# A transformer block with modulated norms: sums moved by some 30 slots, a normalisation moved from ScalarE to GpSimd, and two product chunks of the tail handed out later

## The chip, the cores and the metric

The kernel runs on one core of a Trainium2 chip. A core has five engines that run their own instruction queues and meet through semaphores: TensorE (PE in the profile), VectorE (DVE), ScalarE (ACT), GpSimd (POOL) and SyncE (SP), which here only issues DMAs. The metric is the time of one execution on the device in microseconds (us), as the median of several runs.

## The reference, cut to what matters

One transformer block for 2048 rows of width 512, with six modulation vectors made from a condition `c`:

```python
mod = (_silu(c) @ w_mod).reshape(c.shape[0], 6, 1, -1)
sa, ca, ga, sb, cb, gb = (mod[:, j] for j in range(6))
h = _layernorm(x, axis=-1) * (1 + ca) + sa
x = x + ga * _A_ref(h, A_k_cache, A_v_cache, A_wq, A_wo)      # attention, 32 heads, 8 of K and V, the last 512 keys
h = _layernorm(x, axis=-1) * (1 + cb) + sb
x = x + gb * _B_ref(h, B_w_gate, B_w_up, B_w_down)            # (gelu(h @ w_gate) * (h @ w_up)) @ w_down
```

The change touches three places of it: the making of `sb` and `cb` (modulations 3 and 4), the second layernorm `(x - mean) / sqrt(var + eps)` of the first 1024 rows, and the last down products of the feed-forward.

## The kernel before, in words

Every large product is done in float16 halves: an operand is split into a high and a low part, and `mm3` (lines 85 to 88) issues three 128x512 matmuls for one product of 128 contracted elements. The scale of each operand comes from bounds on its norm, which is why there are many small scale steps.

**Attention** is a list of 512 score tiles, run in a loop over "slots" t = 0 to 511 with a few more at the end. In each slot PE makes the scores of one tile (`ps`), DVE takes their row maximum (`nm`, L945), ACT the exponential (`ee`, L954), and for the tiles of two and three slots ago ACT and DVE make the high and low half of the probabilities `p` (L966 and L971), which a transposing DMA turns into `pt`. PE also takes three further pieces of work from a list in each slot: query products, value products (`po`) and output products (`py`), whose results DVE and ACT turn into `qt`, `ot` and the accumulator `acc` (L705, L706, L914). The first 256 slots serve rows 0 to 1023 (first half), the others the rest (second half). In the first half the weights are also split and stored, in the second most of them are fetched back.

**The order** of this loop is written out by hand: within it each engine executes what the code issues, in the order in which it issues it. Side work has slots: `at(t, f)` and `at(("w", t), f)` put f at the end of slot t, `sched` gives a load and its later steps their slots, and a planner spaces the loads by the free buffers (five `raw` buffers of 256 KB) and issues them on SP, with about one background DMA in a slot. The rest of the feed-forward, behind the loop, is not in hand order: there a scheduler orders the instructions of PE, DVE, ACT and GpSimd; only SP's stay as written.

**Modulation.** For modulations 3, 4 and 5 a column block of `w_mod` is loaded as a 128x512 tile (`wmc`, `mod_load`), and `mod_col` (L135) multiplies it by silu(c) and sums along the row on DVE; for modulation 4 a one is added (L137). When the eight columns of 3 and 4 are there, `mod_max` (L189) takes their largest value and `mod_scale` (two small transposes on PE at L194, then L196 to L211 on DVE) scales them for the feed-forward. Their first readers are the affine steps of the second layernorm.

**Second layernorm.** When the attention output of a 128-row tile of rows 0 to 1023 is complete (`attn_final`), its accumulator is stored to `y1`, and `ln_tile(2, ...)` runs on it in place: `stat` (mean and variance on DVE, the power on GpSimd at L386, one slot later), `norm` (six slots later), `turn` (four transposes on PE at L495, eight slots later), the affine (L503 on ACT), its store to `hs` and the split into the blocks `b` (L521 on ACT, L523 on GpSimd). There are eight such tiles, at slots about 258 to 294.

**Tail.** The feed-forward goes through 28 steps q, each of seven products named by `ORDER` (L1527). Pairs of steps (gate and up) give eight output chunks of six matmuls each (`py<-wo,at`), kept in the list `nexty`; `y_next()` issues one. At four of the seven places of each step one chunk of an earlier pair is issued; what is left is issued behind the last step.

Of the kernel before, what the change touches and what calls it, by code (L numbers as in the profile page):

```python
# [10 lines left out]
F32 = mybir.dt.float32  # L11
F16 = mybir.dt.float16
BF16 = mybir.dt.bfloat16
AF = mybir.ActivationFunctionType
ALU = mybir.AluOpType
AX = mybir.AxisListType

P = 128
# [45 lines left out]
def block_kernel(ctx: ExitStack, tc: tile.TileContext, x, kT, v, wq, wo, wg, wu, wd, cT, wc, wm, out):  # L64
    nc = tc.nc
# [3 lines left out]
    small = ctx.enter_context(tc.tile_pool(name="small", bufs=4))  # L69
# [3 lines left out]
    def tmp(name):  # L73
        return pool.tile([P, 512], F32, tag="e", name=name, bufs=NE)

    def raw(name):
        return pool.tile([P, 512], F32, tag="raw", name=name, bufs=NRAW)
# [4 lines left out]
    def bank(tag, name, bufs):  # L82
        return psum.tile([P, 512], F32, tag=tag, name=name, bufs=bufs)
# [8 lines left out]
    def dma(out_, in_):  # L92
        moved[0] += 1
        nc.sync.dma_start(out_, in_)
# [81 lines left out]
    def col(name, i=0):  # L176
        return ST[name][:, i:i + 1]

    def ts(out, src, a, b=None, op0=ALU.mult, op1=ALU.mult):
        if b is None:  # L180
            nc.vector.tensor_scalar(out, src, a, None, op0=op0)
        else:
            nc.vector.tensor_scalar(out, src, a, b, op0=op0, op1=op1)

    def little(name, n=1, bufs=4, dtype=F32):
        return small.tile([P, n], dtype, tag=name, name=name, bufs=bufs)

    def absmax(out, src):
        nc.vector.tensor_reduce(out, src, axis=AX.X, op=ALU.max, apply_absolute_value=True)  # L189

    def everywhere(out, m, n, fold=True):
        ps = bank("acc", "pst", NACC)
        for i in range(n):
            nc.tensor.transpose(ps[:, i * P:(i + 1) * P], m[:, i:i + 1].to_broadcast([P, P]), ident)  # L194
        src = ps[:, :n * P] if fold else ps[:, :n * P].rearrange("p (n q) -> p n q", n=n)
        nc.vector.tensor_reduce(out, src, axis=AX.X, op=ALU.max)  # L196

    def mod_max(j):
        m = little("mm", 2, 1)
        absmax(m, cols[:, j:j + 2, :])  # L200
        return m

    def mod_scale(j, name, const_, m=None, mid=nop, between=nop):
        m, g, s = m or mod_max(j), little("mg", 2, 1), little("ms", 1, 1)
        everywhere(g, m, 2, False)
        mid()
        nc.vector.tensor_tensor(s, g[:, 0:1], g[:, 1:2], op=ALU.add)
        ts(s, s, FLOOR, RT / TOP13, ALU.max)
        ts(col(name), s, const_)
        between()  # L210
        nc.vector.reciprocal(s, s)  # L211
        ts(cols[:, j:j + 2, :], cols[:, j:j + 2, :], s)
# [23 lines left out]
    def pool_ts(out, src, a, b=1.0, op0=ALU.mult, op1=ALU.mult):  # L236
        nc.gpsimd.tensor_scalar(out, src, a, b, op0=op0, op1=op1)
# [108 lines left out]
    def spilled(gen, key):  # L346
        if (gen, key) not in hs:
            n = KT if key in (0, 1) else 2
            hs[gen, key] = dram.tile([P, n, QB], F32, name=f"hs{gen}_{key}")
        return hs[gen, key]  # L350
# [20 lines left out]
    def ln_cols(key):  # L371
        return (1, 0) if key == "a" else (4, 3)

    def ln_stat(a, st, act=False):
        bn = small.tile([P, 6], F32, name="bn")
        nc.vector.bn_stats(bn, a)
        st["mv"] = small.tile([P, 2], F32, name="mv")
        nc.vector.bn_aggr(st["mv"], bn)
        st["rs"] = small.tile([P, 1], F32, name="rs")
        nc.vector.tensor_scalar(st["rs"], st["mv"][:, 1:2], EPS, None, op0=ALU.add)  # L380
        if act:
            st["nm"] = small.tile([P, 1], F32, name="nmean")
            nc.vector.tensor_scalar(st["nm"], st["mv"][:, 0:1], -1.0, None, op0=ALU.mult)

    def ln_power(st):
        nc.gpsimd.tensor_tensor(st["rs"], st["rs"], nhalf, op=ALU.pow)  # L386
# [58 lines left out]
    def put_off(n, fn):  # L445

        waits_.append([n, fn])
# [17 lines left out]
    def ln_tile(gen, i, src):  # L465
        jsc, jsh = ln_cols("a" if gen < 2 else "f")
        qb, i = divmod(i % (2 * QT), QT)
        st = {}

        def load():  # L470
            if gen == 2:
                st["x"] = src()
            else:
                st["x"] = raw("xs")
                dma(st["x"], src())

        def stat():
            ln_stat(st["x"], st)
            ln_power(st)
            if gen == 2:  # L480
                st["nm"] = small.tile([P, 1], F32, name="nmean")
                pool_ts(st["nm"], st["mv"][:, 0:1], st["rs"], -1.0)

        def norm():
            if gen == 3:
                rs, nm = col("kmax", qb * QT + i), col("kinv", qb * QT + i)
                return nc.scalar.activation(st["x"], st["x"], AF.Identity, bias=nm, scale=rs)
            if gen == 2:
                return nc.scalar.activation(st["x"], st["x"], AF.Identity, bias=st["nm"], scale=st["rs"])
            nc.vector.tensor_scalar(st["x"], st["x"], st["mv"][:, 0:1], st["rs"], op0=ALU.subtract, op1=ALU.mult)  # L490

        def turn():
            st["ps"] = bank("acc", "pln", NACC)
            for dt in range(KT):
                nc.tensor.transpose(st["ps"][:, dt * P:(dt + 1) * P], st["x"][:, dt * P:(dt + 1) * P], ident)  # L495

        def affine(dts):
            if 0 in dts:
                st["f"] = raw("hf") if gen == 2 else tmp("hf")
            f = st["f"]  # L500
            for dt in dts:
                sl = slice(dt * P, (dt + 1) * P)
                nc.scalar.activation(f[:, sl], st["ps"][:, sl], AF.Identity,  # L503
                                     scale=cols[:, jsc, dt:dt + 1], bias=cols[:, jsh, dt:dt + 1])
            if KT - 1 in dts:
                def spill():
                    dma(spilled(gen, qb)[:, :, i * P:(i + 1) * P], f.rearrange("p (k q) -> p k q", k=KT))

                if gen == 3:
                    put_off(3, spill)  # L510
                else:
                    spill()

        def parts(act):
            o = slice(i * P, (i + 1) * P)
            f = st["f"].rearrange("p (k q) -> p k q", k=KT)
            for h, name in enumerate(("b11", "b21") if qb == 0 else (None, "b22")):
                if name:
                    t, src = block(gen, name), f[:, 2 * h:2 * h + 2, :]
                    if act:  # L520
                        nc.scalar.activation(t[:, 0:2, o], src, AF.Copy)  # L521
                    else:
                        nc.gpsimd.tensor_tensor(t[:, 2:4, o], src, t[:, 0:2, o], op=ALU.subtract)  # L523

        more = [lambda: parts(True), lambda: parts(False)] if gen < 3 else []
        return load, [nop if gen == 3 else stat, norm, turn, lambda: affine((0, 1)), lambda: affine((2, 3))] + more
# [170 lines left out]
    def at(key, *fns):  # L697
        later.setdefault(key, []).extend(fns)
# [425 lines left out]
    for dt in range(KT):  # L1124
        sched(6 + dt, (lambda dt=dt: gate_load(dt), [lambda dt=dt: gate_cols(dt)]), ahead=8)
    at(("d", 10), lambda: ts(cols[:, 2, :], gps["ps"][:, 0:KT], 1.0, None, ALU.mult))
    for j, ts_ in ((3, (211, 215, 223, 227)), (4, (213, 217, 225, 229)), (5, (274, 278, 282, 286))):
        for dt in range(KT):
            box = {}
            sched(ts_[dt], (lambda box=box, j=j, dt=dt: box.update(f=mod_load(j, dt)), [lambda box=box: box["f"]()]))  # L1130
    at(11, lambda: mod_row(2))
    mx = {}
    at(("w", 232), lambda: mx.update(m=mod_max(3)))
    at(234, lambda: mod_scale(3, "mf", 1.0, mx["m"]))

    def sched_combos(gen, p, base):
        for k, (load, steps) in enumerate(combos(gen, p, nc.gpsimd if gen or p == 0 else nc.vector, False, 0 if gen else 1 if p else 2, 0 if gen or p else 5)):
# [77 lines left out]
    NQ = 4 * NP  # L1215
# [323 lines left out]
    for i in range(2 * QT):  # L1539
        load, steps = ln_tile(3, i, lambda i=i: y1[2 * QT + i])  # L1540
        q = 7 * (2 + i // 2) + 3 * (i % 2)
# [3 lines left out]
    for p in range(2):  # L1545
        q = 7 * (7 + 2 * p)
# [13 lines left out]
    for q in range(NQ):  # L1560
        n, m = divmod(q, 2)
        its = items(NG + q) if q < 2 else f_items(q)
        for k, pk in enumerate(ORDER):
            if (q, pk) not in f_done:
                all_of(its[pk])
            run(("f", q, k))
            tick()
            if k in (1, 2, 5, 6):
                y_next()
        if m == 1:  # L1570
            for qi, (a, b) in enumerate((("11", "21"), ("12", "22"))):
                for i in range(QT):
                    nexty.append(y_tasks((2 * (n // NP) + qi) * QT + i, [lambda n=n, a=a: A[n, a], lambda n=n, b=b: A[n, b]],
                                         [("f", n, 0), ("f", n, 1)], col("dysc", n % NP), f_final if n % NP == NP - 1 else None))
# [39 lines left out]
```

## Time and profile before

| what | value |
|---|---|
| runs | 1769.34, 1772.45, 1772.27 us; median 1772.27 |
| the profiled execution | 1769.1 us, of which the span of the profile is 1767.3 |
| granted TensorE clock | 1.0 |
| PE waits in all, for `qt` alone | 15.4 us, 12 times |
| the eight normalisations on ACT (L489) | 0.815 us each (median), 708 to 786 us |
| the twelve modulation sums on DVE (L135) | 0.683 us each (median), 1.642 the longest |

All times in the profile are from the start of the span. "Busy" is the time in which an engine has an instruction in work; PE's matmuls overlap, so the 0.38 us of one and the 0.215 us from one start to the next are both right. A group row names line, engine, operation, output <- inputs, shapes and count, then busy us and mean ns, then the idle time in front and who ended it. In a timeline row the numbers are start and duration, and a bracket at the end is the idle time of that engine in front of it, with the releaser. The releaser is inferred; where it had long been done, another was meant.

### The profile page before, as it was taken

The page shows a single profiled execution, that of the slowest core. Times are in us where ns is not written, and L with a number is a line of the kernel's source. Part 1 is how long each engine was busy: PE and PEld are TensorE (multiplying, and loading weights), DVE is VectorE, ACT ScalarE, POOL GpSimd, SP SyncE. Part 2 cuts the span into 40 slices and gives each one's busy share as a digit, 9 for nine tenths or more (in the row PEclk, how much of TensorE's full clock was granted, in tenths as well). Part 3 has the DMA queues.
Part 4 walks back from the last instruction along what each step waited for, and adds up shares of the span by engine and source line. Part 5 has one row for each costly group of instructions (what it writes and reads, how often), then busy time and mean ns, then how long its engine had stood idle before and what let it go on. Part 6 is the DMA issues. An engine that isn't in the chain of part 4 may idle for free.

```text
span 1767.3 us, 25992 instructions
## 1 busy us (share of the span) xinstructions
PE 1730.0 (98%) x8114; PEld 796.3 (45%) x8114; DVE 1447.2 (82%) x2501; ACT 1219.3 (69%) x2830; POOL 882.2 (50%) x1119
## 2 busy tenths in 40 slices
PE   7899999999999999999999999999999999999998
PEld 4444444444444444444444444444444444444443
DVE  7888888888888998888888888888886768767676
ACT  5887787878778777897777777777674555434342
POOL 4879878776788873444565555555520024000000
PEclk9999999999999999999999999999999999999999
DMA  7999999989999997999999999999985643252222
GB/s 230 209 195 210 218 217 200 223 204 221 216 216 227 224 201 145 208 205 234 208 208 208 212 214 204 206 211 214 188 185 131 199 129 114 83 173 90 86 75 75
DMA packets 662122, 327.62 MB, mean 185 GB/s; under 512 B 553056, under 2 KB 575840, under 8 KB 661984
## 3 DMA queue, kind: packets, MB, share of 16 engines
q1 hardware_dynamic: 661696, 325.44, 80.0%
q8 instruction: 64, 1.05, 0.3%
q14 instruction: 74, 0.61, 0.1%
q10 hardware_dynamic: 288, 0.52, 0.1%
HBM read 131.73 MB, written 59.90 MB: 108 GB/s over the span
## 4 chain that ended last, share of the span: by engine, by line
PE 72%; DVE 14%; ACT 8%; issue 3%; POOL 2%; DMA 1%; SPq 0%; ACTq 0%; POOLq 0%; DVEq 0%
PE py L86 7%; PE py L88 7%; PE py L87 7%; DVE p L971 5%; PE ps L86 4%; PE ps L88 4%; PE ps L87 4%; PE po L86 4%; PE po L88 4%; PE po L87 4%; DVE nm L945 3%; PE fa L86 3%; PE fa L88 3%; PE fa L87 3%; ACT ee L954 2%
## 5 line engine op out<-in xcount | busy, mean ns | idle before, releaser
L954 ACT ACTIVATE ee<-ps,nm 128x512 f32<-128x512 f32 x512 | 350.9, 685 | 251.0 <-DVE nm L945 245.6
L971 DVE SCALAR_TENSOR_TENSOR p<-ee,rr,p 128x512 f16<-128x512 f32 x512 | 470.0, 918 | 0.9 <-ACT p L966 0.7
L945 DVE TENSOR_REDUCE nm<-ps 128x1 f32<-128x512 f32 x512 | 349.4, 683 | 77.0 <-PE ps L88 75.5
L966 ACT ACTIVATE p<-ee,rr 128x512 f16<-128x512 f32 x512 | 365.4, 714 | 2.3 <-DMA pt<-p 1.9
L86 PE MATMUL ps<-k,qt 128*128 128x512 f16 x512 | 194.1, 379 | 16.6 <-DVE qt L706 15.4
L86 PE MATMUL py<-wo,ot 128*128 128x512 f16 x512 | 194.1, 379 | 4.4 <-DVE ot L706 4.4
L87 PE MATMUL po<-pt,v 128*128 128x512 f16 x512 | 194.0, 379 | 0.0
L88 PE MATMUL po<-pt,v 128*128 128x512 f16 x512 | 194.0, 379 | 0.0
L87 PE MATMUL py<-wo,ot 128*128 128x512 f16 x512 | 194.0, 379 | 0.0
L88 PE MATMUL py<-wo,ot 128*128 128x512 f16 x512 | 194.0, 379 | 0.0
L86 PE MATMUL po<-pt,v 128*128 128x512 f16 x512 | 194.0, 379 | 0.0
L88 PE MATMUL ps<-k,qt 128*128 128x512 f16 x512 | 194.0, 379 | 0.0
L87 PE MATMUL ps<-k,qt 128*128 128x512 f16 x512 | 193.9, 379 | 0.0
L962 DVE RECIPROCAL rr<-rr 128x2 f32<-128x2 f32 x256 | 41.4, 162 | 99.6 <-ACT rr L959 98.5
L87 PEld LDWEIGHTS <-w 128*128 128x128 f16 x728 | 71.2, 98 | 86.2 <-issue 1.2
L88 PEld LDWEIGHTS <-w 128*128 128x128 f16 x728 | 71.2, 98 | 86.0 <-issue 0.2
L86 PEld LDWEIGHTS <-w 128*128 128x128 f16 x728 | 71.2, 98 | 85.5 <-DVE w L1016 0.3
L914 DVE SCALAR_TENSOR_TENSOR acc<-py,dysc,acc 128x512 f32<-128x512 f32 x112 | 81.6, 747 | 31.5 <-PE py L88 30.5
L954 ACT ACTIVATION_READ_ACCUMULATOR ee<-ps,nm 128x1 f32 x512 | 100.8, 197 | 0.0
L914 DVE SCALAR_TENSOR_TENSOR acc<-py,ysc,acc 128x512 f32<-128x512 f32 x128 | 94.7, 740 | 3.9 <-PE py L88 3.9
L706 DVE SCALAR_TENSOR_TENSOR ot<-po,ot 128x512 f16<-128x512 f32 x128 | 87.0, 680 | 0.0
L86 PE MATMUL py<-wo,at 128*128 128x512 f16 x224 | 84.9, 379 | 1.4 <-DVE at L1263 1.4
(270 smaller groups left out, 3765.9 us busy)
## 6 DMA issues: line engine op xcount, KB each, us to landing
w<-kept SPq DMA_DIRECT2D x123, 256.0 KB, 3.2
wo<-kept SPq DMA_DIRECT2D x60, 256.0 KB, 3.5
raw<-in_wo SPq DMA_DIRECT2D x56, 256.0 KB, 3.1
kept<-stage SPq DMA_DIRECT2D x56, 256.0 KB, 3.3
kept<-w SPq DMA_DIRECT2D x39, 256.0 KB, 3.4
rw<-in_wq SPq DMA_DIRECT2D x38, 256.0 KB, 3.3
hs<-hf SPq DMA_DIRECT2D x32, 256.0 KB, 2.7
pt<-p SPq DMA_TRANSPOSE x512, 3.5
```

The costliest lines, as they stand in the source:

```text
L86: nc.tensor.matmul(ps, llo, rhi, start=first, stop=False, skip_group_check=chain)
L87: nc.tensor.matmul(ps, lhi, rlo, start=False, stop=False, skip_group_check=chain)
L88: nc.tensor.matmul(ps, lhi, rhi, start=False, stop=last, skip_group_check=chain)
L706: return lambda: nc.vector.scalar_tensor_tensor(t[:, 1, :], src, scale, t[:, 0, :], op0=ALU.mult, op1=ALU.subtract)
L914: nc.vector.scalar_tensor_tensor(acc[ti], st["p"], by, acc[ti], op0=ALU.mult, op1=ALU.add)
L945: nc.vector.tensor_reduce(nm, E[t]["ps"], axis=AX.X, op=ALU.max, negate=True)
L954: nc.scalar.activation(e, E[t]["ps"], AF.Exp, bias=E[t]["nm"], scale=1.0, accum_out=sm[:, t % 2:t % 2 + 1])
L962: return lambda: nc.vector.reciprocal(r, r)
L966: nc.scalar.activation(p16[:, 0, :], E[t]["e"], AF.Copy, scale=E[t]["r"])
L971: nc.vector.scalar_tensor_tensor(p16[:, 1, :], E[t]["e"], E[t]["r"], p16[:, 0, :], op0=ALU.mult, op1=ALU.subtract)
```

## The change

It has three parts.

1. The loads and sums of modulations 3 and 4 move from slots 211 to 229 to slots 243 to 257, `mod_max` from 232 to 258 and `mod_scale` from 234 to 260.
2. `norm` of the second layernorm of rows 0 to 1023 is done by GpSimd, in place, as (x - mean) * rs with both as column operands; before, ACT did it as x * rs + nm. The small GpSimd product that made nm = -mean * rs goes.
3. In the last of the 28 steps of the feed-forward, `y_next()` is called at two places (k = 1 and 5) rather than four, so that two chunks stand behind the last product in the program's text.

```diff
@@ ln_tile
         def stat():
             ln_stat(st["x"], st)
             ln_power(st)
-            if gen == 2:
-                st["nm"] = small.tile([P, 1], F32, name="nmean")
-                pool_ts(st["nm"], st["mv"][:, 0:1], st["rs"], -1.0)
...
             if gen == 2:
-                return nc.scalar.activation(st["x"], st["x"], AF.Identity, bias=st["nm"], scale=st["rs"])
+                return pool_ts(st["x"], st["x"], st["mv"][:, 0:1], st["rs"], ALU.subtract, ALU.mult)
@@ modulation
-    for j, ts_ in ((3, (211, 215, 223, 227)), (4, (213, 217, 225, 229)), (5, (274, 278, 282, 286))):
+    for j, ts_ in ((3, (243, 247, 251, 255)), (4, (245, 249, 253, 257)), (5, (274, 278, 282, 286))):
...
-    at(("w", 232), lambda: mx.update(m=mod_max(3)))
-    at(234, lambda: mod_scale(3, "mf", 1.0, mx["m"]))
+    at(("w", 258), lambda: mx.update(m=mod_max(3)))
+    at(260, lambda: mod_scale(3, "mf", 1.0, mx["m"]))
@@ feed-forward steps
-            if k in (1, 2, 5, 6):
+            if k in ((1, 2, 5, 6) if q < NQ - 1 else (1, 5)):
                 y_next()
```

## Prediction, made blind

> **What bounds the kernel now.** I read the page first (busy shares), then the table of what TensorE (PE) waited for, then PE's own timeline at each of those waits, then the other engines at the same places.
>
> ```profile
> span 1767.3 us, 25992 instructions
> ...
> PE 1730.0 (98%) x8114; PEld 796.3 (45%) x8114; DVE 1447.2 (82%) x2501; ACT 1219.3 (69%) x2830; POOL 882.2 (50%) x1119
> ```
>
> PE is busy for 98% of the span, and the change neither adds nor removes a matmul of it. So time can only come out of PE's waits, or be added to them. The table of PE's waits (total us, times, longest):
>
> ```profile
> PE ps L86 <- DVE qt L706: 15.4, 12, 2.7
> PE py L86 <- DVE ot L706: 4.4, 4, 1.7
> ```
>
> A part of this lies in stretches that the change leaves alone. All that PE waited between 569 and 800 us, which it touches, from the timeline (start, duration, then the idle time before it in brackets and what ended it):
>
> ```profile
> 578.04 0.39 PE L86 MATMUL ps<-k,qt 128*128 128x512 f16 x1 [0.33 <-DVE qt L706]
> 602.79 0.38 PE L86 MATMUL qa<-t,x 128*128 128x512 f16 x1 [0.41 <-ACT u L847]
> 605.95 0.39 PE L86 MATMUL py<-wo,ot 128*128 128x512 f16 x1 [1.70 <-DVE ot L706]
> 610.88 0.39 PE L86 MATMUL ps<-k,qt 128*128 128x512 f16 x1 [0.22 <-DVE qt L706]
> 621.97 0.39 PE L86 MATMUL ps<-k,qt 128*128 128x512 f16 x1 [0.56 <-ACT s L847]
> 654.14 0.39 PE L86 MATMUL ps<-k,qt 128*128 128x512 f16 x1 [1.75 <-DVE qt L706]
> 744.48 0.33 PE L495 MATMUL pln<-ident,acc 128*128 128x128 f32 x1 [0.79 <-ACT hf L503]
> 774.87 0.39 PE L86 MATMUL py<-wo,ot 128*128 128x512 f16 x1 [1.02 <-DVE ot L706]
> 788.97 0.33 PE L495 MATMUL pln<-ident,acc 128*128 128x128 f32 x1 [0.73 <-ACT hf L503]
> ```
>
> The first five (3.22 us) fall where the eight moved sums run today, the next one (1.75) between the old and the new place, the last three (2.54) where the normalisation runs. At the very end stands one more, of 1.39 us (part 3). That is all there is to gain: 3.22 + 1.75 + 2.54 + 1.39 = 8.9 us, or 0.5%.
>
> **Part 1: the sums, old place.** VectorE (DVE) sets the first waits. The longest of them, step by step:
>
> ```profile
> 601.41 1.62 DVE L135 SCALAR_TENSOR_TENSOR wmc<-wmc,sbc 128x512 f32<-128x512 f32 x1
> ...
> 603.63 1.65 DVE L971 SCALAR_TENSOR_TENSOR p<-ee,rr,p 128x512 f16<-128x512 f32 x1
> ...
> 605.21 0.68 DVE L706 SCALAR_TENSOR_TENSOR ot<-po,ot 128x512 f16<-128x512 f32 x1
> ```
>
> A sum (L135, 1.62) stands ahead of the `ot` for which PE waits 1.70; without it `ot` is there 1.55 us sooner (601.41 to the 602.96 of the next instruction), and what is left is 0.15. The other four waits are each shorter than the sums in front of them. I take all 3.2 us as gone; nothing else in these slots is late by more than a sum.
>
> **Part 1: the new place.** Slots 243 and 258 are where their row maxima begin, and the load of the stretches is:
>
> ```profile
> 654.67 0.68 DVE L945 TENSOR_REDUCE nm<-ps 128x1 f32<-128x512 f32 x1
> ...
> 691.26 0.69 DVE L945 TENSOR_REDUCE nm<-ps 128x1 f32<-128x512 f32 x1 [1.24 <-PE ps L88]
> ```
>
> ```profile
> 593.00:623.00 30.00, 27.09 (x125) 11.74 (x124) 28.00 (x51) 20.88 (x51) 25.90 (x33) 1.00 0.83 196
> 654.00:692.00 38.00, 37.86 (x176) 17.24 (x177) 31.58 (x55) 26.98 (x65) 18.18 (x20) 1.00 0.78 143
> 740.00:790.00 50.00, 47.46 (x232) 22.65 (x230) 41.33 (x81) 44.99 (x112) 18.65 (x27) 1.00 0.90 205
> ```
>
> (stretch, length, then busy us of PE, weight loads, DVE, ACT, GpSimd, then granted clock, DMA share, GB/s.) In the old place DVE works 28.0 of 30 us; in the new one 31.58 of 38, so 6.4 us are free. What goes in, with the groups of 567 to 623 us:
>
> ```profile
> L135 DVE SCALAR_TENSOR_TENSOR wmc<-wmc,sbc 128x512 f32<-128x512 f32 x8 | 8.6, 1074 | 0.0
> L137 DVE TENSOR_SCALAR cols<-cols 128x1 f32<-128x1 f32 x4 | 0.6, 154 | 0.1
> ```
>
> At the old mean that is 8.6 + 0.6 = 9.2 us, or 2.8 more than is free. But the old mean is stretched by GpSimd: over all twelve sums the row says 676/683/1642 ns,
>
> ```profile
> L135 DVE SCALAR_TENSOR_TENSOR wmc<-wmc,sbc x12: 676/683/1642, 569.0 to 768.3; 128x512 f32<-128x512 f32 x12
> ```
>
> so an undisturbed sum is 0.68, and eight of them with the 0.6 make 6.1, which fits. GpSimd is busy 86% in the old stretch (25.90 of 30) and 48% in the new (18.18 of 38); with the stretching in proportion a sum is 0.68 + 0.39 x 48/86 = 0.90 and the whole 7.8, an overrun of 1.4 us. It is carried as a lag of DVE behind PE. How much lag costs nothing shows at the closing step of the modulation (L189 and L196 to L181), which moves from slot 234 to 260:
>
> ```profile
> 629.96 0.38 PE L86 MATMUL ps<-k,qt 128*128 128x512 f16 x1
> ```
>
> ```profile
> 631.76 0.42 DVE L196 TENSOR_REDUCE mg<-pst 128x2 f32<-128x256 f32 x1
> ...
> 633.85 0.69 DVE L945 TENSOR_REDUCE nm<-ps 128x1 f32<-128x512 f32 x1
> ```
>
> It holds DVE for 2.1 us; the next maximum then begins 3.9 us after the start of its scores, and PE has no wait until 654.14. An overrun of 1.4 us stays below that; with the 2.1 us at slot 260 it may just not. I take 0.8 us of new waits, with 0 and 4.9 (2.8 + 2.1) as ends. Of the 1.75 us at 654.14 I count 0.4 as gone, since the 2.1 us no longer precede it (ends 0 and 1.75). The eight 256 KB loads move too, on SP's queue past the fetches of the next pair's K and V; PE shows no wait for a fetch in either stretch, and the new one has the lowest DMA share of the three (0.78). Nothing for them. Part 1: -3.2 - 0.4 + 0.8 = **-2.8 us** (ends -5.0 and +1.7).
>
> **Part 2: the normalisation.** The rows for the two forms, and for the small product that goes:
>
> ```profile
> L489 ACT ACTIVATE acc<-acc,nmean,rs x8: 800/815/837, 708.3 to 785.5; 128x512 f32<-128x512 f32 x8
> L237 POOL TENSOR_SCALAR nmean<-mv,rs x8: 264/660/722, 697.0 to 772.1; 128x1 f32<-128x1 f32 x8
> L160 POOL TENSOR_SCALAR rw<-rw,wsc x34: 682/697/1243, 51.0 to 730.9; 128x512 f32<-128x512 f32 x34
> ```
>
> ScalarE (ACT) loses 8 x 0.815 = 6.5 us, in a stretch where it is the fullest of the helpers (44.99 of 50). GpSimd loses 8 x 0.66 and gets eight 128x512 in-place operations. No row has that form with two column operands; the nearest is L160, one column and a constant: 0.70, with 0.68 and 1.24 as ends. At 744.48 and 788.97 PE waits for `hf`, and an L489 stands a few steps ahead of it on ACT; it is worth 0.7 us, and 0.1 of each wait is left. At 774.87 the chain goes through ACT and then DVE, with no L489 close by; I count half. Gain: 0.7 + 0.6 + 0.5 = 1.8 (ends 0 and 2.5).
>
> What is late next is GpSimd, which works in order. The built program's order puts the norm of tile 3 behind the three L760, and that of tile 4 behind two L523, before PE's turn:
>
> ```profile
> 739.86 2.65 POOL L760 TENSOR_TENSOR rw<-rw 128x256 f32<-128x256 f32 x3
> ```
>
> ```profile
> 751.63 1.47 POOL L157 TENSOR_TENSOR w<-rw,w 128x512 f16<-128x512 f32 x1
> 753.06 1.75 POOL L523 TENSOR_TENSOR b<-hf,b 128x256 f16<-128x256 f32 x2
> ```
>
> ```profile
> 755.33 0.38 PE L495 MATMUL pln<-ident,acc 128*128 128x128 f32 x2
> ```
>
> Tile 3: 739.86 + 2.65 - 0.7 (the small product gone) + 0.70 = 742.5, before 743.7. Tile 4: 753.06 + 1.75 + 0.70 = 755.5, or 756.05 at 1.24: 0.2 to 0.7 late; I take 0.4. Tile 0, the tightest of the others, stands behind an L157 and has room to 1.24:
>
> ```profile
> 708.51 1.16 POOL L157 TENSOR_TENSOR w<-rw,w 128x512 f16<-128x512 f32 x1
> ```
>
> ```profile
> 712.43 0.60 PE L495 MATMUL pln<-ident,acc 128*128 128x128 f32 x4
> ```
>
> 708.51 + 1.16 + 1.24 = 710.9, before 712.43. The added GpSimd work may also stretch L971 as at 603.63 (1.65), but DVE has 8.7 us free between 740 and 790. Part 2: -1.8 + 0.4 = **-1.4 us** (ends -2.5 and +0.7). A page of the Trainium skill speaks against this part: GPSIMD Engine Reference, section "Elementwise — side-by-side cycle accounting", gives 769 ns for 512 elements in its best loop and calls VectorE the place for such work. By that figure the eight cost 6.2 us rather than 5.6, and the sum above stays, as an estimate; L160's median of 697 ns is the faster of the two.
>
> **Part 3: the two chunks.** The end of the kernel:
>
> ```profile
> 1752.94 0.69 DVE L1260 SCALAR_TENSOR_TENSOR fg<-fg,fa 128x512 f32<-128x512 f32 x1 [0.76 <-PE fa L88]
> ...
> 1754.23 0.69 DVE L1232 TENSOR_TENSOR u<-u,fc 128x512 f32<-128x512 f32 x1
> 1754.84 0.68 DVE L1263 TENSOR_TENSOR at<-fg,at 128x512 f16<-128x512 f32 x1
> ```
>
> ```profile
> 1755.58 0.39 PE L86 MATMUL py<-wo,at 128*128 128x512 f16 x1 [1.39 <-DVE at L1263]
> ```
>
> Two chunks behind the last product would cover these 1.39 us. But this stage's order is the scheduler's, and in the built program it takes the two chunks ahead of the last products again: behind the last `fc` stand 36 `py` matmuls, before and after alike, the first with the same `at` made by L1260, ACT, L1232 and L1263 in that order. What changes is an earlier `fc`, with weights that were loaded long before. **0 us** (ends -1.4 and +0.3).
>
> **The sum:** -2.8 - 1.4 + 0 = -4.2 us. The profiled execution took 1769.1 us (span 1767.3 and 1.8 around it), so 1764.9; the same 4.2 from the median of the runs, 1772.27, gives 1768.1, which I predict. The runs themselves lie 3.1 us apart. A measurement of this kernel can tell about 0.2%, or 3.5 us, from no change.
>
> **The rivals.**
> - *Given back* (0.32): the gain at the old place is real, but the overrun in the new one is the old mean's 2.8 us and tile 4 comes 0.7 late, with the 1.02 and 1.75 us waits untouched. -3.2 + 2.8 - 1.3 + 0.7 = -1.0: 1771.3. For it: DVE's 6.4 free us are barely the cost. Against: PE waits nowhere between 654.14 and 744.48 today.
> - *The new place is worse than the old* (0.12): one mechanism, DVE held up by GpSimd in slots 243 to 262. It decides once a sum takes over 1.2 us: eight then make 10.2 with the 0.6, an overrun of 3.8, about the lag that cost nothing above. At the worst row, 1.64, eight with 0.6 are 13.7, or 7.3 over the free 6.4; PE then waits for `qt` of slot 258 and `ot` of 257 as at 654.14 and 605.95. Net 7.3 - 3.2 - 1.4 = +2.7: 1775.0. For it: in the old place PE waited as soon as DVE was full (28.0 of 30). Against: GpSimd is at 48% in the new. The Trainium skill (SBUF — State Buffer, "Who interferes with whom") holds that a VectorE instruction with two SBUF inputs and a GpSimd one that reads SBUF shut each other out, whichever comes second waiting in full; the trace's 0.68 against 1.64 agrees, and by that rule this rival rests on who comes first.
> - *The tail does what it says, or 654.14 goes as well* (0.12): -4.2 - 1.4 to -4.2 - 1.35, say 1766.7.
>
> **Chances.** Forecast 0.44. It and the last case are faster by over 0.2%, less some 0.04 of the forecast's narrow margin (4.2 against 3.5): faster 0.52, same 0.36 (given back, and that margin), slower 0.12. The range reaches from both best ends (-3.2 - 0.4 - 2.5, from the lowest run 1769.3: 1763.2) to about half of the slower rival: 1763.0 to 1773.5.
>
> **What would show it.** Right: no PE wait between 569 and 640 us; DVE fuller between 654 and 692, with maxima up to 3 us behind their scores and PE waits under 1 us there and around slot 261; the eight in-place operations near 0.7 to 1.2 us; a wait of PE for GpSimd only at the fifth tile; the 1.39 us before `at` unchanged. Wrong: waits for `qt` or `ot` of over 1 us behind slot 243, or several turns waiting for GpSimd.

## The result, and the profile after

The changed kernel takes 1766.49 us (median of 7 runs, 1764.06 to 1768.29) where the kernel before takes 1772.45 (7 runs beside them, 1769.34 to 1773.13). The medians are 6.0 us apart, or 0.3%. The ratio of the two kernels is 0.9969, 95% interval 0.9957 to 0.9980, which is 3.5 to 7.6 us; it is estimated from the runs and is not the quotient of the two medians. The forecast was 4.2 us and 1768.1.

The page of the changed kernel, its own execution of 1768.29 us:

```profile
span 1766.5 us, 25988 instructions
...
PE 1733.8 (98%) x8114; PEld 797.5 (45%) x8114; DVE 1448.4 (82%) x2501; ACT 1214.5 (69%) x2822; POOL 891.6 (50%) x1119
```

This span is only 0.8 us below that of before, although the medians are 6.0 apart. One profile against one other doesn't measure such a change; below it is read in stretches. First the waits, from PE's table (total us, times, longest) and from its timeline:

```profile
PE pln L492 <- POOL acc L237: 2.2, 2, 1.1
```

```profile
650.04 0.39 PE L86 MATMUL ps<-k,qt 128*128 128x512 f16 x1 [0.63 <-DVE qt L703]
701.40 0.39 PE L86 MATMUL ps<-k,qt 128*128 128x512 f16 x1 [0.41 <-DVE qt L703]
741.63 0.66 PE L492 MATMUL pln<-ident,acc 128*128 128x128 f32 x4 [1.14 <-POOL acc L237]
753.67 0.66 PE L492 MATMUL pln<-ident,acc 128*128 128x128 f32 x4 [1.02 <-POOL acc L237]
1754.77 0.39 PE L86 MATMUL py<-wo,at 128*128 128x512 f16 x1 [1.39 <-DVE at L1260]
```

(Lines behind 482 are three lower than before's.) Between 569 and 640 us no wait is left. That of 1.75 us at 654.14 is 0.63. A small one of 0.41 stands behind the moved scale step. The three of the normalisation, two for `hf` and one for `ot`, have gone, but two turns now wait for GpSimd, tiles 3 and 4, with 2.16 us together. The tail's 1.39 is as it was.

To compare executions whose starts differ I cut each between the starts of the scores of the same slots: 0, 30, 205, 245, 265, 300, 511, and the last product. Windows of before (stretch, length, then busy us of PE, weight loads, DVE, ACT, GpSimd, then granted clock, DMA share, GB/s), for slots 0 to 30, 205 to 245, 245 to 265, 265 to 300, 300 to 511, and 511 to the end:

```profile
26.11:101.91 75.80, 66.07 (x329) 32.00 (x330) 65.15 (x118) 62.84 (x154) 55.23 (x66) 1.00 0.87 195
...
549.49:656.74 107.25, 101.54 (x470) 45.24 (x469) 97.49 (x175) 79.56 (x193) 86.60 (x97) 1.00 0.96 224
656.74:707.25 50.51, 50.51 (x236) 22.90 (x235) 43.77 (x78) 36.45 (x88) 21.76 (x27) 1.00 0.77 149
707.25:802.41 95.16, 92.62 (x446) 43.93 (x445) 80.33 (x151) 82.51 (x203) 41.62 (x57) 1.00 0.95 206
802.41:1334.22 531.81, 530.33 (x2475) 240.50 (x2474) 452.32 (x767) 402.80 (x976) 274.02 (x344) 1.00 0.96 206
1334.22:1763.14 428.92, 425.95 (x1988) 194.88 (x1987) 300.30 (x460) 186.43 (x314) 36.94 (x46) 1.00 0.37 116
```

The same six of the changed kernel:

```profile
25.65:103.47 77.82, 69.16 (x330) 33.10 (x331) 66.12 (x118) 62.84 (x154) 54.66 (x66) 0.96 0.86 190
...
551.00:652.64 101.64, 100.33 (x468) 45.14 (x467) 86.52 (x148) 78.93 (x193) 83.52 (x97) 1.00 0.96 217
652.64:704.00 51.36, 50.95 (x238) 23.04 (x237) 50.48 (x101) 35.88 (x86) 20.66 (x24) 1.00 0.87 181
704.00:798.67 94.67, 92.51 (x446) 43.83 (x445) 83.27 (x154) 78.20 (x197) 56.50 (x58) 1.00 0.95 209
798.67:1331.69 533.02, 530.65 (x2475) 240.38 (x2474) 453.59 (x768) 403.04 (x976) 273.46 (x344) 1.00 0.96 205
1331.69:1762.34 430.65, 426.60 (x1989) 194.76 (x1987) 300.37 (x460) 186.89 (x314) 36.99 (x46) 1.00 0.37 115
```

In slots 205 to 300, all that parts 1 and 2 touch, the change gains 5.61 - 0.85 + 0.49 = 5.25 us. Against that this one execution lost 2.02 us in slots 0 to 30, where the granted clock is 0.96 rather than 1.00 and nothing is changed, and 2.94 behind slot 300. That is how 5.25 became 0.8. It was the slowest of the seven runs of the changed kernel, while before's profiled execution (1769.1) lay below all seven of its.

DVE is now fuller in the new place (50.48 of 51.36 us) than it was in the old one (97.49 of 107.25), and PE waits 0.41 there. The two groups that the change moved or made: the eight moved sums among the groups of 650 to 705 us (busy us, mean ns), then both by line, engine, operation, minimum/median/maximum ns, first and last start:

```profile
L135 DVE SCALAR_TENSOR_TENSOR wmc<-wmc,sbc 128x512 f32<-128x512 f32 x8 | 6.9, 859 | 0.0
```

```profile
L135 DVE SCALAR_TENSOR_TENSOR wmc<-wmc,sbc x12: 677/684/1640, 652.3 to 765.5; 128x512 f32<-128x512 f32 x12
```

```profile
L237 POOL TENSOR_SCALAR acc<-acc,mv,rs x8: 2064/2077/2583, 707.0 to 780.3; 128x512 f32<-128x512 f32 x8
```

The eight sums take 6.9 us where they took 8.6: 859 ns in the mean rather than 1074, close to the 0.90 of the forecast. One of them still took 1.64, where three of the eight took over 1.5 in the old place. The normalisation takes 2.08 us on GpSimd, three times the 0.70 of the forecast.

### The profile page after: what moved, and what is told of

The parts are those of the page before. It is cut to its first block, busy times and chain, and to the rows that moved or that the text cites. A ratio compares the mean times of both kernels' runs of the same rounds, so it can differ in the third digit from the quotient of the medians.

```text
span 1766.5 us, 25988 instructions
## 1 busy us (share of the span) xinstructions
PE 1733.8 (98%) x8114; PEld 797.5 (45%) x8114; DVE 1448.4 (82%) x2501; ACT 1214.5 (69%) x2822; POOL 891.6 (50%) x1119
## 4 chain that ended last, share of the span: by engine, by line
PE 67%; DVE 17%; ACT 8%; issue 3%; POOL 3%; DMA 2%; SPq 0%; POOLq 0%; DVEq 0%; ACTq 0%
PE py L86 7%; PE py L88 7%; PE py L87 7%; DVE p L968 5%; PE ps L86 4%; PE ps L88 4%; PE ps L87 4%; PE po L86 4%; PE po L87 4%; PE po L88 4%; DVE nm L942 3%; PE fa L86 3%; PE fa L88 3%; PE fa L87 3%; ACT ee L951 2%
```

## The experiments

My theory after the result: part 1 carries the whole gain, because VectorE's time in the sums made PE wait. Part 2 is worth about nothing, because its operation takes 2.08 us and makes two waits in place of three. Part 3 is worth nothing, because the scheduler undoes it. The rivals: part 2 carries a share of the gain; or part 1's gain is that of the moved loads or of the scale step, not of the sums.

All twelve runs, with the stretches of their profiles beside the times. "Before" is the median of the kernel before, run beside the other on the same chip.

| kernel | us | before | ratio, 95% interval | slots 205-245 | 245-265 | 265-300 |
|---|---|---|---|---|---|---|
| before | | | | 107.25 | 50.51 | 95.16 |
| changed kernel | 1766.49 | 1772.45 | 0.9969, 0.9957-0.9980 | 101.64 | 51.36 | 94.67 |
| part 1 alone | 1765.20 | 1770.51 | 0.9975, 0.9965-0.9985 | 101.81 | 50.72 | 95.16 |
| part 2 alone | 1770.73 | 1770.51 | 1.0001, 0.9992-1.0009 | 106.98 | 50.50 | 94.63 |
| part 3 alone | 1770.70 | 1770.51 | 1.0005, 0.9996-1.0014 | 106.92 | 50.51 | 95.16 |
| scale step alone | 1769.76 | 1770.51 | 0.9996, 0.9987-1.0005 | 105.86 | 50.73 | 95.16 |
| before without the sums | 1767.61 | 1772.45 | 0.9976, 0.9965-0.9986 | 102.93 | 50.51 | 95.64 |
| changed kernel again | 1765.98 | 1771.96 | 0.9965, 0.9953-0.9978 | 102.00 | 51.03 | 94.69 |
| norm in two passes | 1768.01 | 1771.96 | 0.9977, 0.9968-0.9986 | 101.20 | 51.39 | 96.54 |
| norm two slots earlier | 1765.86 | 1771.96 | 0.9964, 0.9951-0.9976 | 101.50 | 51.42 | 94.33 |
| tail held | 1764.95 | 1771.96 | 0.9959, 0.9945-0.9972 | 101.95 | 51.05 | 94.71 |
| norm as multiply, add | 1765.90 | 1772.45 | 0.9965, 0.9953-0.9977 | 102.07 | 51.12 | 95.36 |
| parts 1 and 3, tail held | 1765.62 | 1771.19 | 0.9968, 0.9955-0.9980 | 101.29 | 50.72 | 95.16 |
| all, multiply and add, tail held | 1765.40 | 1771.19 | 0.9965, 0.9953-0.9977 | 101.51 | 50.72 | 95.02 |

The times of single runs spread by 2 to 5 us (once 7), so differences under 2 us are read in the stretches. How well these repeat shows where kernels run the same code. Slots 205 to 245 took 106.92 to 107.25 us in the three kernels with nothing of part 1, and 101.20 to 102.07 in the nine with all of it. Slots 265 to 300 took 95.16 in five of the six with the normalisation on ScalarE and 95.64 in the sixth. So one profile's stretch can be off by 0.3 to 0.9 us.

### Each part alone

Part 1 alone is the second hunk of the change, part 2 alone the first, part 3 alone the third.

> The kernel before with part 1 alone: the eight loads and sums at slots 243 to 257 and the closing scale step at 260. Theory (part 1 carries the whole gain): 4 to 5.5 us faster than before, with no PE wait between 569 and 640 us, under 1 us left of the 1.75 us wait at 654, a small new wait of some 0.4 us near slot 261, and the 1.02 and 0.73 us waits at 775 and 789 us still there. Rival (the normalisation on GpSimd carries half of it): 2 to 3 us faster.

> The kernel before with part 2 alone: the eight normalisations on GpSimd with two column operands. Theory: the operation takes 2.08 us as in the changed kernel, PE loses the 0.79, 1.02 and 0.73 us waits at 744, 775 and 789 us and gets two waits for GpSimd of about 1.1 us each at tiles 3 and 4: the time is within 0.5 us of before. Rival: the waits for GpSimd were due to the sums next to them, then they are absent here and it is 2 us or more faster.

> The kernel before with part 3 alone: two calls in the last step rather than four. Theory: the scheduler takes the two chunks ahead of the last products all the same, the wait of 1.39 us near the end stays, and the time is that of before within 0.3 us. Rival: the other order of the last products is worth something by itself, 1 us either way.

Part 1 alone gives 0.9975 of before; in its profile 5.44 us come from slots 205 to 245 and 0.21 go at the new place:

```profile
551.25:653.06 101.81, 100.35 (x469) 45.08 (x468) 86.32 (x148) 78.98 (x193) 83.67 (x97) 1.00 0.96 218
653.06:703.78 50.72, 50.72 (x237) 23.14 (x236) 49.82 (x103) 36.13 (x86) 21.67 (x26) 1.00 0.92 183
```

PE has no idle time at all in slots 245 to 265 (50.72 of 50.72) with DVE at 49.82. So the 0.21 is not a wait: it is the two small transposes of the scale step, PE's own work, which now falls here (with the scale step alone, below, the row of this stretch has 238 matmuls where before's has 236). Part 2 alone changes nothing (1.0001): its own stretch is 0.53 us shorter, with waits for GpSimd of 1.14 and 1.03 us where 0.79, 1.02 and 0.73 stood. Part 3 alone changes nothing (1.0005) and leaves its wait at 1.39. So part 1 carries the gain.

Parts 1 and 2 together lose more at slot 260 (0.85, and 0.52 in the second run) than part 1 alone (0.21). The rows say why. In the changed kernel, DVE and GpSimd at 693 us:

```profile
693.25 1.28 DVE L968 SCALAR_TENSOR_TENSOR p<-ee,rr,p 128x512 f16<-128x512 f32 x1
```

```profile
693.27 2.66 POOL L757 TENSOR_TENSOR rw<-rw 128x256 f32<-128x256 f32 x3
```

and with part 1 alone:

```profile
693.33 0.73 DVE L971 SCALAR_TENSOR_TENSOR p<-ee,rr,p 128x512 f16<-128x512 f32 x1
```

```profile
694.16 2.33 POOL L760 TENSOR_TENSOR rw<-rw 128x256 f32<-128x256 f32 x3
```

Without the small product that made nm, GpSimd begins its three operations 0.02 us behind the start of DVE's `p` rather than 0.83, that is 0.8 us sooner and beside it rather than behind it, and `p` takes 0.55 us longer just ahead of the scale step. That is read from rows, not separated by a run; among the kernels with all of part 1, those that keep the small product have 50.72 there in three profiles of four (51.12 in the other), and those without it 51.03 to 51.42.

### Which step of part 1: the scale step, or the sums

The first kernel moves only `mod_max` and `mod_scale`:

```diff
-    at(("w", 232), lambda: mx.update(m=mod_max(3)))
-    at(234, lambda: mod_scale(3, "mf", 1.0, mx["m"]))
+    at(("w", 258), lambda: mx.update(m=mod_max(3)))
+    at(260, lambda: mod_scale(3, "mf", 1.0, mx["m"]))
```

> The kernel before with only the closing scale step of the modulations moved, from slots 232 and 234 to 258 and 260; loads and sums stay at slots 211 to 229. Theory: the five waits between 569 and 640 us stay (3.2 us) since the sums make them; the 1.75 us at 654 us shrinks only if the 2.1 us of the scale step made it: then 1 to 1.7 us faster, less some 0.4 us at the new place. Rival: the lag that the sums themselves leave makes the 654 wait, then it stays at 1 us or more and the time is that of before.

```profile
549.99:655.85 105.86, 101.33 (x468) 44.88 (x467) 96.25 (x168) 79.85 (x193) 86.41 (x97) 1.00 0.97 226
655.85:706.58 50.73, 50.73 (x238) 23.14 (x237) 43.75 (x83) 36.03 (x87) 20.50 (x26) 1.00 0.75 146
```

It gains 1.06 to 1.39 us at the old place (against the 106.92 and 107.25 of kernels that leave it alone) and loses 0.22 at the new one; the five waits stay, 3.4 us in all. The 0.22 is again PE's time for the two transposes (238 matmuls rather than 236, no idle time in either), and that much of the gain at the old place is the same two transposes gone from there. The new place costs the same 0.2 with and without the sums beside it: the sums themselves cost nothing there. The wait at 654 us is 0.63 or 0.64 in all profiles with the scale step moved, and 0.78, 0.79, 1.62 or 1.75 without. So it varies by 1 us where nothing near it was changed, and what the scale step made of the 1.75 isn't shown by that wait alone. The medians, 0.75 us apart, don't tell this kernel from before (0.9996).

The second kernel takes the sums away and leaves their loads:

```diff
     def mod_load(j, dt):
         t = raw("wmc")
         dma(t, wc[j, :, dt, :])
+        if j < 5:
+            return lambda: nc.vector.tensor_scalar(cols[:, j, dt:dt + 1], t[:, 0:1], 1.0, None, op0=ALU.mult)
         return lambda: mod_col(j, dt, t, sbc)
```

> The kernel before with the eight sums of modulations 3 and 4 replaced by copies of one column, at their old slots; loads, largest value and scale step stay where they were. It leaves those sums out, so it shows what the old place costs and nothing else. Theory: VectorE's time in the sums makes the five waits between 569 and 640 us, so none over 0.3 us is left there, slots 205 to 245 take 4 to 5.5 us less than the 106.9 to 107.3 of before, and the time is 4 to 5 us below before. Rival: the eight loads that stood in SP's queue and in the weight buffers make part of the waits; then 1 us or more of them stays, since the loads are still there.

```profile
549.39:652.32 102.93, 100.55 (x470) 45.37 (x469) 88.38 (x163) 79.02 (x193) 83.86 (x97) 1.00 1.00 233
```

```profile
649.72 0.39 PE L86 MATMUL ps<-k,qt 128*128 128x512 f16 x1 [1.62 <-DVE qt L708]
```

All five waits of 569 to 640 us are gone with the loads still there, so VectorE's time made them and the loads cost nothing. The wait at 654 us, behind the scale step, stays (1.62), so the sums don't make it. The sums make 4.32 us (3.99 against the 106.92 of part 3 alone) and the scale step 1.06 to 1.39, together 5.1 to 5.7; part 1 gives 5.1 to 5.4. The 4.32 also show the price of a wait: PE's idle time falls by 3.33 (5.71 to 2.38) and its busy time by 0.99 for the same 470 matmuls. Five waits fewer give 0.2 each. Most of that is the matmul ahead of a wait: it runs its 0.38 us to the end, where otherwise the next one starts 0.215 after it did.

### What part 2 could have given

Four kernels: the changed kernel again as their base; its normalisation as two operations of one column each; its normalisation two slots sooner; and, later, x times rs plus nm, which again has two columns but no subtraction.

```diff
-return pool_ts(st["x"], st["x"], st["mv"][:, 0:1], st["rs"], ALU.subtract, ALU.mult)
+return (pool_ts(st["x"], st["x"], st["mv"][:, 0:1], 1.0, ALU.subtract, ALU.mult), pool_ts(st["x"], st["x"], st["rs"]))
```

```diff
-zip((1, 6, 8, 9, 10, 12, 13), steps)
+zip((1, 4, 8, 9, 10, 12, 13), steps)
```

```diff
+            if gen == 2:
+                st["nm"] = small.tile([P, 1], F32, name="nmean")
+                pool_ts(st["nm"], st["mv"][:, 0:1], st["rs"], -1.0)
...
-return pool_ts(st["x"], st["x"], st["mv"][:, 0:1], st["rs"], ALU.subtract, ALU.mult)
+return pool_ts(st["x"], st["x"], st["rs"], st["nm"], ALU.mult, ALU.add)
```

> The changed kernel once more, with the line numbers of the kernel before, as the base for the three that follow. Theory (part 1 gives its 5.2 us of slots 205 to 265, part 2 about 0.8 of which 0.6 is lost to part 1's scale step at slot 260, part 3 nothing): 1764 to 1767 us, 4.5 to 6 us faster than before, two waits of PE for GpSimd of 1.0 to 1.2 us near 741 and 753 us. Rival (the parts' single results simply add up): 3.5 us faster.

> The changed kernel with each normalisation as two GpSimd operations of one column operand each (minus the mean, then times rs). Theory: the second column operand is what makes one operation take 2.08 us, one-column forms take 0.69; the pair takes 1.4 us, PE's two waits for GpSimd shrink from 1.14 and 1.02 to 0.5 and 0.4 us, and the time is about 1 us below the changed kernel's. Rival: the subtraction, or working in place, makes it slow; then each pass takes over 1 us, the pair 2 us or more, and nothing is gained.

> The changed kernel with the normalisation handed to GpSimd four slots behind the tile's end rather than six, ahead of the operations that stood in front of it for tiles 3 and 4. Theory: those two waits are GpSimd's order, so both go (2.2 us, and the restart of PE's pipeline behind each): 2 to 2.7 us below the changed kernel. Rival: what is put behind is then late itself, or holds VectorE up, and PE gets other waits between 700 and 800 us: less than 1 us gained.

> The changed kernel with the normalisation on GpSimd as x times rs plus nm, two column operands again, with the small product that makes nm back in its place. Two theories of the 2.08 us: the subtraction makes it slow, since in the two-pass kernel the pass that subtracts took 2.00 us and the pass that multiplies 0.70; then this form takes 0.70 to 0.75 us. Or two arithmetic steps of different kinds make it slow, whichever they are; then it takes about 2.08 us again. By the first, PE's two waits for GpSimd (1.14 and 1.03 us) shrink to 0 for tile 3 and under 0.7 for tile 4, as the prediction had them, and the time is 1 to 2 us below the changed kernel's 1765.98; by the second it is 0.5 to 1.5 us above it.

The base repeats the result (0.9965). It doesn't tell its two theories apart by time: 6.0 us between medians, with an interval of 3.9 to 8.3.

The two passes refuted me on the form. The groups of that kernel:

```profile
L237 POOL TENSOR_SCALAR acc<-acc,mv x8: 1990/2002/2505, 705.3 to 779.9; 128x512 f32<-128x512 f32 x8
L237 POOL TENSOR_SCALAR acc<-acc,rs x8: 695/697/1204, 707.4 to 782.0; 128x512 f32<-128x512 f32 x8
```

The pass with the subtraction takes 2.00 us with one column, the other 0.70: the second column isn't the cost, nor is working in place. Together they take 2.7 us, and slots 265 to 300 grow by 1.85. Multiply and add settle it:

```profile
L237 POOL TENSOR_SCALAR acc<-acc,rs,nmean x8: 761/767/1272, 707.0 to 780.4; 128x512 f32<-128x512 f32 x8
```

Two columns, two different steps, 0.77 us. The subtraction is what costs 1.3 us, here as the first step with a column. The Trainium skill (GPSIMD Engine Reference, "Elementwise — side-by-side cycle accounting") has 769 ns for 512 elements in the best loop; this form agrees at 767, the subtraction at 2077 doesn't. Which other operations share that no run here shows.

But the cheap form gains nothing either: 95.36 us, 0.2 more than with ScalarE, and no gain in time over the changed kernel (1765.90 beside 1772.45, 1765.98 beside 1771.96). Its PE timeline:

```profile
740.81 0.63 PE L495 MATMUL pln<-ident,acc 128*128 128x128 f32 x4 [0.89 <-ACT rr L959]
752.47 0.66 PE L495 MATMUL pln<-ident,acc 128*128 128x128 f32 x4 [0.68 <-POOL acc L237]
772.24 0.39 PE L86 MATMUL py<-wo,ot 128*128 128x512 f16 x1 [1.19 <-DVE ot L706]
```

2.76 us, with the operation at the size that the forecast gave it. The first is the wait of before's 744.48 (0.79), with no L489 left on ACT. What ACT now waits for ahead of it, from DVE's and ACT's timelines of this kernel:

```profile
738.56 0.68 DVE L725 TENSOR_TENSOR qd<-u,qc 128x512 f32<-128x512 f32 x1
```

```profile
739.28 0.69 ACT L705 ACTIVATE qt<-qd,qsc 128x512 f16<-128x512 f32 x1
```

`qt` starts 0.04 us behind the end of DVE's `qd` (738.56 + 0.68), and `hf` stands behind `qt`. In before `qd` ended at 742.54 and this `qt` began at 743.04: only 0.5 us of slack lay under the 0.8 of L489, and then DVE is the limit.

```profile
741.86 0.68 DVE L725 TENSOR_TENSOR qd<-u,qc 128x512 f32<-128x512 f32 x1
```

```profile
743.04 0.69 ACT L705 ACTIVATE qt<-qd,qsc 128x512 f16<-128x512 f32 x1
```

That alone would leave some 0.3 us of the 0.79, not 0.89. The rest is that DVE itself comes later than before. Counted from the start of slot 265's scores, `qd` ends at 35.29 us in before (742.54 - 707.25), at 35.76 here (739.24 - 703.48) and at 35.43 in the last kernel of the table, which has the same normalisation and a wait of 0.56. Most of the 0.47 is one row. Here, on DVE and GpSimd:

```profile
732.83 1.17 DVE L971 SCALAR_TENSOR_TENSOR p<-ee,rr,p 128x512 f16<-128x512 f32 x1
```

```profile
731.71 1.75 POOL L523 TENSOR_TENSOR b<-hf,b 128x256 f16<-128x256 f32 x2
```

and in before:

```profile
736.64 0.73 DVE L971 SCALAR_TENSOR_TENSOR p<-ee,rr,p 128x512 f16<-128x512 f32 x1
```

```profile
734.88 1.75 POOL L523 TENSOR_TENSOR b<-hf,b 128x256 f16<-128x256 f32 x2 [0.22 <-ACT b L521]
```

In before GpSimd's L523 had ended when `p` began; with a normalisation ahead of it in GpSimd's queue it runs beside `p`. This is read from rows, not separated by a run.

The third wait shows still better in the kernel with the early normalisation, where no turn waits for GpSimd. Its stretch is 94.33, only 0.36 below its base, not 2 us:

```profile
771.89 0.39 PE L86 MATMUL py<-wo,ot 128*128 128x512 f16 x1 [1.36 <-DMA pt<-p]
```

A `pt` is named, but the `ot` that this product reads ended on DVE at 771.83 (771.15 + 0.68), 0.06 us before it. DVE had stood idle for ACT's `rr`, and ACT's queue ahead of it holds no normalisation:

```profile
768.39 0.60 ACT L847 ACTIVATE u<-qa 128x512 f32<-128x512 f32 x1
768.87 0.64 ACT L216 ACTIVATE junk<-rw 128x512 f16<-128x512 f32 x1
...
769.48 0.81 ACT L503 ACTIVATE hf<-pln,cols 128x128 f32<-128x128 f32 x2
770.16 0.22 ACT L959 ACTIVATE rr<-sm 128x2 f32<-128x2 f32 x1
```

```profile
770.41 0.17 DVE L962 RECIPROCAL rr<-rr 128x2 f32<-128x2 f32 x1 [1.45 <-ACT rr L959]
...
771.15 0.68 DVE L706 SCALAR_TENSOR_TENSOR ot<-po,ot 128x512 f16<-128x512 f32 x1
```

DVE waits 1.45 us for a `rr` that stands behind two L503, as it does in before. In the changed kernel the wait at `ot` was absent because PE had just lost 2.16 us to GpSimd and came later. So between slots 265 and 300 the pair DVE and ACT limits PE, and most of a wait taken away comes back at the next place: every form and place of the normalisation gives 94.3 to 95.4 us, except the two passes with 96.5.

### What part 3 could have given

Here the scheduler is told to keep two chunks behind the last product:

```diff
-        nc.tensor.matmul(ps, lhi, rhi, start=False, stop=last, skip_group_check=chain)
+        lastmm[0] = nc.tensor.matmul(ps, lhi, rhi, start=False, stop=last, skip_group_check=chain)
...
+    ins = lastmm[0]
+    ins = getattr(ins, "ins", ins)
+    with tc.issue_after(ins):
+        y_next()
+        y_next()
     while nexty:
         y_next()
```

> The changed kernel with its two held-back chunks truly behind the last product of the feed-forward, by telling the scheduler so. Theory: the wait of 1.39 us before the last down product goes, since twelve matmuls (2.6 us) then lie between the last product and that one: 1.4 to 1.6 us below the changed kernel. Rival: the chunks are taken from a place where they cover something else, or the last products begin no earlier; then a wait of the same size turns up elsewhere behind 1700 us and the time stays.

> Part 1 and the tail with its two chunks truly held back, and no part 2: the normalisation stays on ScalarE. Theory: the gains of part 1 (5.2 us of slots 205 to 265) and of the held tail (0.7 us net: 1.39 gone, 0.69 new) are separate and add up, and part 2 is worth nothing beside them: 5.5 to 6.5 us below before. Rival: part 2 is worth its 0.5 us of slots 265 to 300 or more in the run times; then this one is 0.5 to 1 us slower than its sister with part 2.

> All three parts, with the normalisation on GpSimd in the cheap form (times rs, plus nm: 0.77 us in place of 2.08) and the two chunks truly held back. Theory: as its sister without part 2, within 0.7 us, because slots 265 to 300 took 95.4 us with the cheap form and 95.2 with the normalisation on ScalarE: VectorE and ScalarE are what is late there. Rival: the time freed on ScalarE shows once the tail is held, and it is 1 us or more faster than its sister.

The 1.39 us are gone, and 0.69 turn up ahead of the last `fa`, which the held chunks no longer cover. In the kernel without part 2:

```profile
1743.04 0.38 PE L86 MATMUL fa<-t,x 128*128 128x512 f16 x1 [0.69 <-ACT u L848]
```

Counted back from the last matmul, the last 300 matmul rows take 65.38 us in all three kernels with the held tail and 66.08 to 66.10 in all others: 0.7 gained, halfway between the theory and its rival. That is 0.04%, and no interval here tells it from nothing; the profile of the first of the three even lost 2.0 us at a `fa` at 1418.7 us, in another place, and ran at half clock for 3.4 us behind it. With and without part 2 the two last kernels differ by 0.2 us. No version tried is faster than the changed kernel by more than the intervals.

## Why the prediction came out, and which steps failed

- **Part 1, old place** (-3.2): the mechanism is shown by the run without the sums, the term was too small. I priced the five waits at their idle time; they cost 4.0 to 4.3, since each also costs some 0.2 us of PE's busy time. So "that is all there is to gain" was too low as well.
- **The wait at 654.14** (-0.4): right in direction, too small in size. The run with only the scale step moved gains 1.1 to 1.4 there, of which 0.2 is its two transposes, paid again at the new place.
- **New place** (+0.8): right in direction. 0.2 for the scale step's transposes, 0 for the sums, and up to 0.6 more beside part 2, from GpSimd operations that begin 0.8 us sooner. The mean of a sum, put at 0.90, is 0.86. DVE was filled almost wholly at no cost: with part 1 alone its row maxima began up to 3.4 us behind the start of their scores (slot 252), and PE had no wait.
- **Part 2** (-1.4): wrong, 0.5 in the stretch and 0 in time. The step "the nearest is L160, one column and a constant: 0.70, with 0.68 and 1.24 as ends" took the duration from a row with the same shape and another operation; a subtraction takes 2.08. Hence tile 4 waits longer and tile 3 waits too. For tile 3 the step "- 0.7 (the small product gone)" failed besides: with 2.08 the sum there gives 743.9, 0.2 late, but the wait is 1.14. In the changed kernel the three L757 begin only 0.3 us sooner, counted from slot 265 (DVE's `rs`, which GpSimd waits for, comes 0.5 later), and last longer than the 2.65: 3.23 us.

```profile
736.29 3.23 POOL L757 TENSOR_TENSOR rw<-rw 128x256 f32<-128x256 f32 x3
```

The step "it is worth 0.7 us, and 0.1 of each wait is left" held for the second of its two waits, which is gone, and failed for the first: with the operation at 0.77 us it is 0.89, because DVE's `qd` left only 0.5 us of slack and comes 0.5 later. And half of the wait at 774.87 wasn't to be had, since no normalisation stands ahead of its `rr`.
- **Part 3** (0): right; the wait is 1.38 or 1.39 in every kernel without the hold.
- **The sum**: -2.8 - 1.4 + 0 came to -4.8 - 0.5 + 0 in the stretches of the changed kernel: 2.0 us too little in part 1 and 0.9 too much in part 2 partly cancel, which is luck, and the total is 1.1 off. The medians, 6.0 apart, are within their interval of that (3.5 to 7.6).
- **The rivals**: nothing was given back at the new place beyond 0.9, and what held DVE up there (a sum of 1.64 us, a `p` of 1.28) made PE wait 0.41 at most. The eight sums' 1.64 us, on which "the new place is worse" rests, occurs once among the eight, whose mean is 0.86.

What stays open: behind slot 300 the five kernels with both parts 1 and 2 and the old tail took 961.8 to 963.7 us, the kernels with one of the parts or none 960.4 to 962.2. The difference of means, 1.2 us, consists of small waits at changing places. In the changed kernel PE waits 0.62 us for ACT's `u` at 1403.23, behind an `xs` for whose load ACT had stood idle 4.35 us. ACT waits there in before too (3.55), and PE doesn't. Whether PE's earlier arrival brings these waits out, or chance, I didn't separate.

## What to carry to other kernels

Side work off a full engine pays where that engine ends the critical engine's waits; then each wait counts with some 0.2 us beside its idle time, and the place to move it to need not be empty, only tolerant of lag. Taking one instruction out of a queue pays only as far as the next engine's slack, so read the row that would be late next before booking the whole wait, and look at what shifts on the engine that takes the instruction over. Price an operation from a row with the same arithmetic, not only the same shape, and compare changes of a few us by stretches between the same points, over several executions.

## What the runs showed of the hardware

- A GpSimd scalar operation on 128x512 f32 takes 0.70 us for multiply, multiply, 0.77 for multiply, add with two columns, and 2.00 to 2.08 with a subtraction as its first step.
- The granted clock falls to half for 3.41 us at a time. That happens once or twice within the first 100 us in 11 of the 14 profiles, in none of the other three, and once more at 1419 us in the first kernel with the held tail. Within a profile the starts lie whole multiples of 3.41 us apart (26.16 and 87.60 us in the changed kernel, 18 times 3.413). Counted on that grid, each of the 20 follows a stretch in which PE stood idle for 57 to 81%; four stretches of 57 to 59% and all below went without. So what decides, in these profiles, is how much of PE's waiting (1.7 to 2.8 us at a time) falls into one stretch of the grid. Two stretches of the changed kernel, with a wait of 1.69 us in the first:

```profile
22.74:26.16 3.42, 1.37 (x7) 0.31 (x4) 3.10 (x7) 2.13 (x5) 1.14 (x2) 1.00 0.95 327
26.16:29.57 3.41, 3.41 (x10) 1.31 (x9) 2.66 (x8) 2.06 (x4) 0.65 (x2) 0.50 0.47 151
```

The same wait in before, whose grid lies otherwise: 50% idle rather than 60%, and no half clock behind it:

```profile
24.32:27.73 3.41, 1.72 (x9) 0.71 (x9) 3.08 (x8) 1.34 (x4) 0.56 (x1) 1.00 0.89 316
```

Slots 0 to 30 take 75.8 us without such a stretch (before), 76.8 with one (the changed kernel again), 77.8 with two: 1 us each, so two of them are a third of the gain measured here. The runs' own granted clocks show it too: of the 31 runs of before beside the single parts, the five at 1.000 took 1768.6 us in the mean, the nine at 0.999 took 1770.0, the sixteen at 0.998 took 1771.0.
